# Attention with beacons, then a multiplicative feed-forward: the order of the weight loads, of the weight fusion and of the first two batches

## The chip, the cores and the metric

One Trainium2 chip, one core. The metric is device time of one launch in microseconds (us), the median of repeated runs. Everything below runs in one program: five engines (TensorE or PE, VectorE or DVE, ScalarE or ACT, GpSimd or POOL, SyncE or SP), each with its own instruction queue, and DMA queues that are fed from POOL and from SP.

## The reference

There are 8 batches of 8 heads with 576 positions of 64 elements, and 16 beacon positions in front of keys and values. Attention is causal over the positions, and the beacons are open to all. Its output, with the heads side by side, is the token matrix x of 4608 rows and 512 columns of a feed-forward without any nonlinearity but a product:

```python
k_all = np.concatenate([beacon_k, k], axis=2)
v_all = np.concatenate([beacon_v, v], axis=2)
scores = scale * np.matmul(q, k_all.transpose(0, 1, 3, 2))
scores = np.where(causal, -1000000000.0, scores)
a = np.exp(scores - scores.max(-1, keepdims=True))
a /= a.sum(-1, keepdims=True) + 1e-09
attn = np.matmul(a, v_all)
x = attn.transpose(0, 2, 1, 3).reshape(B * S, H * D)
h = (x @ w1) * (x @ w2) @ w3
out = h @ w_out
```

w1 and w2 are 512 x 1024, w3 is 1024 x 1024, w_out is 1024 x 512. All inputs and the output are float32.

## The kernel before

**Attention.** A batch is worked through in eight steps, two for each pair of heads (`t`), the even one for the first half of the column groups, the odd one for the second (lines 340 to 411). A step consists of `scores` (L351, eight or fourteen matmuls of 64 rows, two heads in two halves of the array), two `exps` on ScalarE (L360), one or two masks on VectorE (L372), `values` (L389, six or twenty-four matmuls of 65 columns; the 65th column of v is one and gives the sum), and a reciprocal and a multiplication on VectorE (L397, L398) that write the normalised rows into x16. Scores lie transposed (keys on partitions), so that the exponentials feed `values` without a transpose.

**Layout of q and k.** Batches 0 and 1 take a path of their own: `load_pair` brings float32 pairs of heads into the tile `st` (L138; batch 0 from SP's queue, batch 1 from POOL's), `cast_pair` casts them on VectorE (L157), and `pe_transpose_pair` transposes them on PE (L171), with the copy of qT on VectorE and that of kT on ScalarE (L177). Batches 2 to 7 are loaded by POOL with a cast to float16 (L104, L113) and transposed by DMAs that SP issues (`transpose_qk`, L128 and L129), five chunks of q and five of k. The rows of x are transposed on PE for batches 0 and 1 (`pe_transpose_x`, L187) and by SP's DMAs later (L409).

**Feed-forward.** w3 @ w_out is computed once, as Wt (`fuse`: for each of eight row tiles eight transposes of w3, L254, a copy on VectorE, L256, eight matmuls of 512 columns, L264, and a copy to float16 on ScalarE, L273). Then x is handled in nine chunks of 512 rows. `ff_ab` has 64 matmuls of 512 columns (L284): eight times a group of four for w1, whose result ScalarE copies into a_sb (L295), and a group of four for w2, which VectorE multiplies with it into gT (L297). `ff_out` has 32 matmuls with Wt (L305), four copies to an output tile `ot` on VectorE (L315, three buffers), and four output DMAs from SP (L316). All products go through the three PSUM buffers of the tile `pm`, which the transposes on PE use as well. w3 is loaded into columns of xT that batches from 4 on will fill (L240).

**Order.** The order on every engine is that of the program text. The feed-forward is a generator, `stream`, that yields after each of its matmuls (64 for the fusion, 96 for each chunk, 928 in all), and `emit_ff(n)` takes the next n of them. The list `fill` says how many are taken in each step. The main loop (L453 to L494) writes scores and the first exponential of step s + 1, then values of step s, up to eight matmuls of the feed-forward, the second exponential and the first mask of step s + 1, the rest of the fill, and the second mask. The last lines of a step add loads of v for the next batch and of q and k for the one after it (at the first step of a batch) and the transposes by DMA (steps 1 to 5).

At the start, POOL's queue holds v of batch 0, w_out, w3, w1 and w2, then q and k of batch 1 in `st`, its v, and q and k of batch 2. Batch 0's attention runs one step ahead of its values. Eight matmuls of the fusion follow step 6 and the other 56 step 7, with the transposes of batch 0's x between; then the first 28 matmuls of the product of chunk 0 surround the transposes of batch 1's pairs. Batch 1 takes 58 more in its steps, batches 2 to 7 take 536, and the remainder follows the last step:

```python
LEFT = 50
n_first = 28
n_kept = 10
n_second = 96 - n_first - n_kept
...
rest, n = n_kept + 6 * 96 - LEFT, NS - 2 * NSB
```

Of the kernel before, what the change touches and what calls it, by code (L numbers as in the profile page):

```python
# [39 lines left out]
def kernel(  # L40
# [81 lines left out]
    def load_v(b, jt):  # L122
        load_kv(b, jt, v, beacon_v, vas[b % NB2][:, jt, :, 0:64])
# [8 lines left out]
    early_qk, early_b = {}, {}  # L132

    def load_pair(b, t):
        engine = nc.gpsimd if b else nc.sync
        for i, src in enumerate((q, k)):
            st = early.tile([P, 2, RUN * D], FP32, name="st")
            engine.dma_start(  # L138
                st[:NR], src[b, ds(2 * t, 2)].rearrange("h (p j) d -> p h (j d)", j=RUN)
            )  # L140
            early_qk[b, t, i] = st
        if t == 0:
            bst = bkp.tile([Nb, H, D], FP32, name="bst")
            engine.dma_start(bst, beacon_k[b].rearrange("h n d -> n h d"))
            early_b[b] = bst

    o16s = {}
# [1 line left out]
    def cast_pair(b, t):  # L149
        if t == 0:  # L150
            b16 = bkp.tile([Nb, DM], FP16, name="b16")
            nc.vector.tensor_copy(b16, early_b[b].rearrange("p h d -> p (h d)"))
            early_b[b] = b16
        o16s[t] = []
        for i in range(2):
            o16 = tiny.tile([P, RUN, P], FP16, name=f"o16_{i}")
            nc.vector.tensor_copy(  # L157
                o16[:NR].rearrange("p j (h d) -> p h j d", h=2),
                early_qk[b, t, i][:NR].rearrange("p h (j d) -> p h j d", j=RUN),
            )  # L160
            o16s[t].append(o16)

    def pe_transpose_pair(b, t):
        qT, kT = qTs[b % NB2], kTs[b % NB2]
        for o16, dst, off, copy in (
            (o16s[t][0], qT, 0, nc.vector.tensor_copy),
            (o16s[t][1], kT, Nb, nc.scalar.copy),
        ):
            pt = psM.tile([P, 1024], FP16, name="pm")
            for j in range(RUN):  # L170
                nc.tensor.transpose(pt[:, ds(j * NR, NR)], o16[:NR, j, :], ident[:NR, :NR])  # L171
            if off:
                nc.tensor.transpose(
                    pt[:, ds(S, Nb)], early_b[b][:, ts(t, P)], ident[:Nb, :Nb]
                )
                copy(dst[:, t, 0:Nb], pt[:, ds(S, Nb)])
            copy(  # L177
                dst[:, t, ds(off, S)].rearrange("p (i j) -> p i j", j=RUN),
                pt[:, 0:S].rearrange("p (j i) -> p i j", j=RUN),
            )  # L180

    def pe_transpose_x(b):
        for i in range(NJT):
            pt = psM.tile([P, NT, P], FP16, name="pm")
            n = QTN[i]
            for t in range(NT):
                nc.tensor.transpose(  # L187
                    pt[:, t, 0:n], x16s[b][:n, i, ts(t, P)], ident[:n, :n]
                )
            dst = xT[:, :, ds(b * S + QT0[i], n)]  # L190
            if i % 2:
                nc.scalar.copy(dst, pt[:, :, 0:n])
            else:
                nc.vector.tensor_copy(dst, pt[:, :, 0:n])

    nc.vector.memset(ident, 1.0)
    nc.vector.memset(MA, 1.0)
# [35 lines left out]
        )  # L233
    for c in range(NJT):
        load_v(0, c)
    wo_v = moe_w_out.rearrange("(a c p) n -> a p c n", p=P, c=2)
    for a in range(4):
        nc.gpsimd.dma_start(wo16[:, ds(2 * a, 2), :], wo_v[a])

    w316 = xT[:, :, ds(M // 2, 2 * DF)].rearrange("p a (c r) -> p a c r", c=2)  # L240
    for kt in range(NFT):
        nc.gpsimd.dma_start(w316[:, kt // 2, kt % 2], moe_w3[ts(kt, P), :])
    for c in range(4):
        for i, w in enumerate((moe_w1, moe_w2)):
            nc.gpsimd.dma_start(
# [4 lines left out]
    def fuse():  # L250
        def w3_transposed(kt):
            pt = psM.tile([P, NFT, P], FP16, name="pm")
            for rt in range(NFT):
                nc.tensor.transpose(pt[:, rt, :], w316[:, kt // 2, kt % 2, ts(rt, P)], ident)  # L254
            wT = wp.tile([P, NFT, P], FP16, name="wT")
            nc.vector.tensor_copy(wT, pt)  # L256
            return wT

        wT = w3_transposed(0)
        for kt in range(NFT):  # L260
            nxt = w3_transposed(kt + 1) if kt + 1 < NFT else None
# [12 lines left out]
            wT = nxt  # L274
            yield
# [64 lines left out]
    def scores(s):  # L340
        b, t, half = s // (2 * NT), (s // 2) % NT, s % 2
        if half == 0:
            pTs[s // 2] = ptp.tile([P, 2, PW], FP16, name="pT")
        qT, kT = qTs[b % NB2], kTs[b % NB2]
        pss[s] = []
        for g in (2 * half, 2 * half + 1):
            ps = psS.tile([P, 2, 512], FP32, name="ps")
            pss[s].append(ps)
            for jt, q0, n, col in GROUPS[g]:
                for hh in range(2):  # L350
                    nc.tensor.matmul(  # L351
                        ps[:, hh, ds(col, n)],
                        kT[ds(hh * 64, 64), t, ts(jt, P)],
                        qT[ds(hh * 64, 64), t, ds(q0, n)],
                    )
# [64 lines left out]
    fill[6] = 8  # L420
    for s in range(NSB, 2 * NSB):
        fill[s] = n_second * (s - NSB + 1) // NSB - n_second * (s - NSB) // NSB
    rest, n = n_kept + 6 * 96 - LEFT, NS - 2 * NSB
    for s in range(2 * NSB, NS):
        fill[s] = rest * (s - 2 * NSB + 1) // n - rest * (s - 2 * NSB) // n

    cast_pair(0, 0)
# [12 lines left out]
    constants(1)  # L440
    for i in range(NB2):
        nc.vector.memset(k16s[i][64:128, 4, :], 0.0)
        nc.vector.memset(q16s[i][64:128, 4, :], 0.0)
    for t in range(2):
        load_pair(1, t)
    for c in range(NJT):
        load_v(1, c)
    for t in range(2, NT):
        load_pair(1, t)
    for c in range(NJT):  # L450
        load_q(2, c)
        load_k(2, c)
    for s in range(NS):  # L453
        b, r = s // NSB, s % NSB
        if s == NSB - 1:
            values(s)
            emit_ff(16)
            pe_transpose_x(0)
            emit_ff(64 - emitted)
            cast_pair(1, 0)  # L460
            for t in range(NT):
                emit_ff(n_first // NT)
                pe_transpose_pair(1, t)
                if t + 1 < NT:
                    cast_pair(1, t + 1)
            emit_ff(64 + n_first - emitted)
            scores(s + 1)
            for j in range(2):
                exps(s + 1, j)
                mask(s + 1, j)  # L470
            continue
# [12 lines left out]
        if s == 2 * NSB - 1:  # L484
            pe_transpose_x(1)
        if 1 <= b < B - 1:
            if r == 0:
                for c in range(NJT):
# [37 lines left out]
```

## Time and profile before

| | |
|---|---|
| median of 8 runs | 326.35 us (323.6 to 329.66) |
| the profiled execution | 323.6 us |
| its span, first to last instruction | 321.6 us |
| PE, DVE, ACT, POOL busy | 290.7, 168.3, 157.8, 114.0 us |
| granted clock of TensorE | 1.00 |
| first product of the feed-forward (L284) | 50.4 us |
| first scores of batch 1 | 61.7 us |
| first values of batch 2 | 89.4 us |
| last matmuls of attention | about 262.8 us |
| read from and written to HBM | 39.32 MB, 9.44 MB |

Times in the trace count from the first instruction of the span. A line of the page's second part is the span in 40 slices of 8.04 us; a digit is the busy share in tenths. A line of the table of windows has the window, its length, then for PE, PE's weight loads, DVE, ACT and POOL the busy time and the number of instructions, then TensorE's granted clock, the DMA share (both kinds of queue added, so it can exceed 1) and GB/s. A line of the chain of waits has start, length, and what the end of the program hung on in that time. A line of the timeline has start, length, engine, line of the kernel, operation, output<-inputs and count; in square brackets stands the idle time before it and what ended it.

### The profile page before, as it was taken

Reading aid. Unit: us, or ns where it says so; the run is one execution under the profiler, and the core shown is the slowest. Engines: PE = TensorE matmul, PEld = TensorE weight load, DVE = VectorE, ACT = ScalarE, POOL = GpSimd, SP = SyncE. Lnnn points to the kernel's source line nnn. Section 1 sums busy time; section 2 is a strip of 40 time slices with the busy share of each in tenths; the row PEclk is TensorE's granted clock in tenths of the full one; section 3 lists DMA queues with packets and bytes.
Section 4 is the critical chain, followed back from the end, with each engine's and each line's share of the span. In section 5 each row is a group of like instructions: output and inputs, shape, how many; then the busy total and the mean of one; then the engine's idle time right before and its main releaser. Section 6 shows DMA issues by size and latency. Waiting matters only on the chain.

```text
span 321.6 us, 6961 instructions
## 1 busy us (share of the span) xinstructions
PE 290.7 (90%) x2800; PEld 151.6 (47%) x2800; DVE 168.3 (52%) x387; ACT 157.8 (49%) x229; POOL 114.0 (35%) x152
## 2 busy tenths in 40 slices
PE   1787799698999995999999999899999989999995
PEld 1565554344554452445454545454445544444442
DVE  4756435655655553555654655555645653343342
ACT  1575424577466653556466556554764452230320
POOL 8545569955593067305910960320000000000000
PEclk9999999999999999999999999999999999999999
DMA  8999999999999979997999999997451112202103
GB/s 190 212 208 205 196 222 202 135 128 139 154 188 145 132 82 178 172 151 88 197 171 170 112 207 169 119 163 143 88 75 67 65 40 62 107 0 88 42 2 130
DMA packets 155824, 42.97 MB, mean 134 GB/s; under 512 B 142976, under 2 KB 149632, under 8 KB 155792
## 3 DMA queue, kind: packets, MB, share of 16 engines
q0 software_dynamic: 102912, 19.67, 77.0%
q1 hardware_dynamic: 52880, 22.85, 39.5%
q8 instruction: 22, 0.36, 0.5%
q14 instruction: 10, 0.08, 0.1%
HBM read 39.32 MB, written 9.44 MB: 152 GB/s over the span
## 4 chain that ended last, share of the span: by engine, by line
PE 59%; DMA 21%; ACT 5%; DVE 4%; POOL 4%; issue 3%; SPq 1%; DVEq 0%; POOLq 0%
PE pm L284 29%; PE pm L305 16%; PE pv L389 8%; DMA w<-in_moe_w_dram 6%; PE ps L351 6%; ACT pT L360 3%; DMA k<-in_k_dram 3%; DMA va<-in_v_dram 3%; DMA xT<-in_moe_w_dram 3%; DMA qT<-q 2%; DMA out_dram<-ot 2%; POOL va L113 2%; DMA st<-in_k_dram 2%; ACT a_sb L295 2%; DVE gT L297 2%
## 5 line engine op out<-in xcount | busy, mean ns | idle before, releaser
L284 PE MATMUL pm<-xT,w 128*128 128x512 f16 x576 | 132.8, 379 | 1.4 <-DMA xT<-x 1.3
L360 ACT ACTIVATE pT<-ps 128x736 f16<-128x736 f32 (+3 forms) x128 | 105.9, 864 | 35.8 <-PE ps L351 35.1
L295 ACT ACTIVATE a_sb<-pm 128x512 f32<-128x512 f32 x72 | 43.0, 597 | 85.7 <-PE pm L284 83.8
L284 PEld LDWEIGHTS <-w 128*128 128x128 f16 x576 | 53.4, 98 | 60.4 <-issue 2.4
L297 DVE TENSOR_TENSOR gT<-pm,a_sb 128x512 f16<-128x512 f32 x72 | 49.7, 690 | 43.8 <-PE pm L284 42.6
L305 PE MATMUL pm<-Wt,gT 128*128 128x512 f16 x288 | 66.4, 379 | 0.0
L113 POOL DMA_DIRECT2D va<-in_v_dram x40 | 34.8, 880 | 68.4 <-PE pv L389 63.6
L351 PE MATMUL ps<-qT,kT 64*128 64x80 f16 (+3 forms) x704 | 40.3, 237 | 9.3 <-ACT pT L360 7.8
L389 PE MATMUL pv<-va,pT 128*128 128x65 f16 x960 | 42.6, 197 | 5.5 <-DVE pT L372 4.9
L389 PEld LDWEIGHTS <-pT 128*128 128x128 f16 x960 | 34.4, 99 | 15.9 <-DVE pT L372 9.9
L305 PEld LDWEIGHTS <-gT 128*128 128x128 f16 x288 | 27.0, 98 | 29.8 <-DVE gT L297 0.2
L397 DVE RECIPROCAL rd<-pv 128x4 f32<-128x4 f32 x64 | 12.1, 190 | 52.8 <-PE pv L389 52.7
L351 PEld LDWEIGHTS <-kT 64*128 64x128 f16 x704 | 21.8, 97 | 37.4 <-issue 33.5
L315 DVE TENSOR_SCALAR ot<-pm 128x512 f32<-128x512 f32 x36 | 24.8, 690 | 24.6 <-PE pm L305 20.0
L398 DVE TENSOR_TENSOR x<-pv,rd 128x256 f16<-128x256 f32 x64 | 31.4, 491 | 2.4
L104 POOL DMA_DIRECT2D q<-in_q_dram x30 | 26.0, 865 | 6.2 <-DMA va<-in_v_dram 2.8
L113 POOL DMA_DIRECT2D k<-in_k_dram x30 | 26.1, 870 | 5.4 <-DMA q<-in_q_dram 2.3
L372 DVE TENSOR_TENSOR pT<-pT,MB 128x512 f16<-128x512 f16 x64 | 19.2, 325 | 5.8 <-ACT pT L360 5.8
L171 PE MATMUL pm<-ident,o 96*128 96x96 f16 x96 | 7.6, 242 | 9.8 <-DVE o L157 8.2
L264 PE MATMUL pm<-wo,wT 128*128 128x512 f16 x64 | 15.0, 379 | 0.4 <-DVE wT L256 0.4
L372 DVE TENSOR_TENSOR pT<-pT,MA 128x480 f16<-128x480 f16 x32 | 12.7, 398 | 1.4 <-ACT pT L360 1.4
L273 ACT CAST Wt<-pm 128x512 f16<-128x512 f32 x8 | 4.7, 587 | 16.2 <-PE pm L264 16.2
(41 smaller groups left out, 94.9 us busy)
## 6 DMA issues: line engine op xcount, KB each, us to landing
out_dram<-ot SPq DMA_DIRECT2D x36, 256.0 KB, 2.7
va<-in_v_dram POOLq DMA_DIRECT2D x24, 128.0 KB, 6.6
q<-in_q_dram POOLq DMA_DIRECT2D x24, 128.0 KB, 8.0
k<-in_k_dram POOLq DMA_DIRECT2D x18, 128.0 KB, 8.8
xT<-in_moe_w_dram POOLq DMA_DIRECT2D x8, 256.0 KB, 10.1
w<-in_moe_w_dram POOLq DMA_DIRECT2D x8, 256.0 KB, 10.2
st<-in_q_dram SPq DMA_DIRECT2D x4, 288.0 KB, 5.4
st<-in_k_dram SPq DMA_DIRECT2D x4, 288.0 KB, 6.4
```

What stands on the lines that cost most here:

```text
L104: nc.gpsimd.dma_start(q16s[b % NB2][:rows, c, :].rearrange("s (h d) -> s h d", h=H), q[b, :, ds(c * P, rows), :].rearrange("h s d -> s h d"),)
L113: nc.gpsimd.dma_start(dst[ds(p0, rows)], src[b, :, ds(s0, rows), :].rearrange("h s d -> s h d"))
L284: nc.tensor.matmul(pm, w12[:, kt, ds(i * DF + kf * P, P)], xT[:, kt, ds(mc * 512, 512)], start=(kt == 0), stop=(kt == NKT - 1),)
L295: nc.scalar.activation(a_sb, pm, AF.Copy, scale=GS)
L297: nc.vector.tensor_tensor(gT[:, kf, :], pm, a_sb, ALU.mult)
L305: nc.tensor.matmul(pm, gT[:, kf, ts(mt, P)], Wt[:, kf, :], start=(kf == 0), stop=(kf == NFT - 1),)
L315: nc.vector.tensor_scalar(ot, pm, float(1.0 / GS), None, ALU.mult)
L351: nc.tensor.matmul(ps[:, hh, ds(col, n)], kT[ds(hh * 64, 64), t, ts(jt, P)], qT[ds(hh * 64, 64), t, ds(q0, n)],)
L360: nc.scalar.activation(pT[:, :, ds(GO[g], GW[g])], pss[s][j][:, :, 0 : GW[g]], AF.Exp, scale=scale)
L372: nc.vector.tensor_tensor(blk, blk, m.unsqueeze(1).to_broadcast([P, 2, n]), ALU.mult)
L389: nc.tensor.matmul(pv[:, 2 * n + hh, 0:65], pT[:, hh, ds(col, P)], va[:, jt, 2 * t + hh, 0:65], start=(jn == 0), stop=(jn == len(BLK[i]) - 1),
L398: nc.vector.tensor_tensor(x16[:, ds(tiles[0], ni), ds(t * P, P)].rearrange("p i (h d) -> p i h d", h=2), pv[:, 0 : 2 * ni, 0:64].rearrange ...
```

## The change

The change moves loads, the fusion and parts of the first two batches.

- **Loads.** After v of batch 0, POOL's queue holds w1 and w2, v of batch 1, q and k of batch 2, v of batch 2, and only then w_out and w3, followed by q and k of batch 3. Batch 1's pairs are loaded by SP's queue, once a one-element memset on VectorE has written each `st` tile; these memsets stand after step 1 of batch 0.
- **Order of the products.** The generator first yields the 64 matmuls of `ff_ab` for chunk 0, then for chunk 1, then the fusion, then both `ff_out`, then chunks 2 to 8 as before. 30 of chunk 0's matmuls surround the transposes of batch 1's pairs, 34 lie in batch 1's steps, 594 in batches 2 to 7, and 270 follow. In the fusion the next row tile's transposes are written after the fourth matmul rather than ahead of the first.
- **Batch 0.** Scores and exponentials run two steps ahead of the values, with no fusion between.
- **Spin.** 32 matmuls of zeros into a `pm` tile that nobody reads: ten at the start, two ahead of each of scores 0, scores 1, the eight values of batch 0 and the transposes of its x.
- **Small ones.** The copy of qT of batch 0's pair 1 moves to ScalarE; four memsets of the rest rows of q16 and k16 move from VectorE to POOL.

```diff
     def load_pair(b, t):
-        engine = nc.gpsimd if b else nc.sync
         for i, src in enumerate((q, k)):
             st = early.tile([P, 2, RUN * D], FP32, name="st")
-            engine.dma_start(
+            if b:
+                nc.vector.memset(st[0:1, 0, 0:1], 0.0)
+            nc.sync.dma_start(
...
-            (o16s[t][0], qT, 0, nc.vector.tensor_copy),
+            (o16s[t][0], qT, 0, nc.vector.tensor_copy if b or t != 1 else nc.scalar.copy),
...
+    def spin(n):
+        pm = psM.tile([P, 512], FP32, name="pm")
+        for _ in range(n):
+            nc.tensor.matmul(pm, zeros[:, 0:P], zeros)
...
     for c in range(NJT):
         load_v(0, c)
-    wo_v = moe_w_out.rearrange("(a c p) n -> a p c n", p=P, c=2)
-    for a in range(4):
-        nc.gpsimd.dma_start(wo16[:, ds(2 * a, 2), :], wo_v[a])
-
-    w316 = xT[:, :, ds(M // 2, 2 * DF)].rearrange("p a (c r) -> p a c r", c=2)
-    for kt in range(NFT):
-        nc.gpsimd.dma_start(w316[:, kt // 2, kt % 2], moe_w3[ts(kt, P), :])
+    for i in range(NB2):
+        nc.gpsimd.memset(k16s[i][64:128, 4, :], 0.0)
+        nc.gpsimd.memset(q16s[i][64:128, 4, :], 0.0)
     for c in range(4):
         for i, w in enumerate((moe_w1, moe_w2)):
...
-            nxt = w3_transposed(kt + 1) if kt + 1 < NFT else None
...
+                if rt == 3 and kt + 1 < NFT:
+                    nxt = w3_transposed(kt + 1)
...
     def stream():
+        gTs = []
+        for mc in range(2):
+            gTs.append((yield from ff_ab(mc)))
         yield from fuse()
-        for mc in range(M // 512):
+        for mc in range(2):
+            yield from ff_out(mc, gTs[mc])
+        for mc in range(2, M // 512):
             gT = yield from ff_ab(mc)
             yield from ff_out(mc, gT)
...
-    LEFT = 50
-    n_first = 28
-    n_kept = 10
-    n_second = 96 - n_first - n_kept
+    LEFT = 270
+    n_first = 30
+    n_second = 64 - n_first
...
+    spin(10)
     cast_pair(0, 0)
     pe_transpose_pair(0, 0)
     cast_pair(0, 1)
-    scores(0)
-    for j in range(2):
-        exps(0, j)
+    spin(2)
+    ahead(0)
     pe_transpose_pair(0, 1)
     cast_pair(0, 2)
-    for j in range(2):
-        mask(0, j)
+    masks(0)
+    spin(2)
+    ahead(1)
     pe_transpose_pair(0, 2)
     cast_pair(0, 3)
+    masks(1)
     pe_transpose_pair(0, 3)
     constants(1)
...
+    for s in range(NSB):
+        if s + 2 < NSB:
+            ahead(s + 2)
+        spin(2)
+        values(s)
+        if s + 2 < NSB:
+            masks(s + 2)
+        if s == 1:
+            for t in range(NT):
+                load_pair(1, t)
+    for c in range(NJT):
+        load_v(2, c)
+    wo_v = moe_w_out.rearrange("(a c p) n -> a p c n", p=P, c=2)
+    for a in range(4):
+        nc.gpsimd.dma_start(wo16[:, ds(2 * a, 2), :], wo_v[a])
+
+    w316 = xT[:, :, ds(M // 2, 2 * DF)].rearrange("p a (c r) -> p a c r", c=2)
+    for kt in range(NFT):
+        nc.gpsimd.dma_start(w316[:, kt // 2, kt % 2], moe_w3[ts(kt, P), :])
+    cast_pair(1, 0)
+    spin(2)
+    pe_transpose_x(0)
+    for t in range(NT):
+        emit_ff(n_first // NT)
+        pe_transpose_pair(1, t)
+        if t + 1 < NT:
+            cast_pair(1, t + 1)
+    emit_ff(n_first - emitted)
+    ahead(NSB)
+    masks(NSB)
+    for s in range(NSB, NS):
```

`ahead(s)` writes `scores(s)` and both `exps(s, j)`, `masks(s)` both masks. The branch of the main loop for the last step of batch 0 goes, and v of batch 2 is no longer loaded in batch 1's first step.

More of the change, by code (lines that the diff above doesn't have):

```diff
@@ L143, in load_pair @@
             bst = bkp.tile([Nb, H, D], FP32, name="bst")
-            engine.dma_start(bst, beacon_k[b].rearrange("h n d -> n h d"))
+            nc.sync.dma_start(bst, beacon_k[b].rearrange("h n d -> n h d"))
             early_b[b] = bst
@@ L194, in pe_transpose_x @@
                 nc.vector.tensor_copy(dst, pt[:, :, 0:n])
+    zeros = const.tile([P, 512], FP16, name="zeros")
+    nc.vector.memset(zeros, 0.0)
+    def spin(n):
+        pm = psM.tile([P, 512], FP32, name="pm")
+        for _ in range(n):
+            nc.tensor.matmul(pm, zeros[:, 0:P], zeros)
     nc.vector.memset(ident, 1.0)
@@ L414, with ahead, masks @@
     NS = B * NSB
-    LEFT = 50
-    n_first = 28
-    n_kept = 10
-    n_second = 96 - n_first - n_kept
+    LEFT = 270
+    n_first = 30
+    n_second = 64 - n_first
     fill = [0] * NS
-    fill[6] = 8
     for s in range(NSB, 2 * NSB):
         fill[s] = n_second * (s - NSB + 1) // NSB - n_second * (s - NSB) // NSB
-    rest, n = n_kept + 6 * 96 - LEFT, NS - 2 * NSB
+    rest, n = 64 + 96 * (M // 512) - 64 - LEFT, NS - 2 * NSB
     for s in range(2 * NSB, NS):
         fill[s] = rest * (s - 2 * NSB + 1) // n - rest * (s - 2 * NSB) // n
+    def ahead(s):
+        scores(s)
+        for j in range(2):
+            exps(s, j)
+    def masks(s):
+        for j in range(2):
+            mask(s, j)
+    spin(10)
     cast_pair(0, 0)
@@ L429 @@
     cast_pair(0, 1)
-    scores(0)
-    for j in range(2):
-        exps(0, j)
+    spin(2)
+    ahead(0)
     pe_transpose_pair(0, 1)
     cast_pair(0, 2)
-    for j in range(2):
-        mask(0, j)
+    masks(0)
+    spin(2)
+    ahead(1)
     pe_transpose_pair(0, 2)
     cast_pair(0, 3)
+    masks(1)
     pe_transpose_pair(0, 3)
     constants(1)
[L441 to L445, printed above, removed]
     for c in range(NJT):
         load_v(1, c)
-    for t in range(2, NT):
-        load_pair(1, t)
     for c in range(NJT):
@@ L452 @@
         load_k(2, c)
-    for s in range(NS):
-        b, r = s // NSB, s % NSB
[L455 to L471, printed above, removed]
+    for s in range(NSB):
[28 more added lines that the diff above has]
+    for s in range(NSB, NS):
+        b, r = s // NSB, s % NSB
         if s + 1 < NS:
@@ L487 @@
             if r == 0:
-                for c in range(NJT):
+                for c in range(NJT if b > 1 else 0):
                     load_v(b + 1, c)
```

## The prediction

> **What bounds the kernel now.** I read the page's 40 slices first, then the table of windows, then the chain of waits and the timeline of TensorE. The slices say where the time is lost:
>
> ```profile
> PE   1787799698999995999999999899999989999995
> DMA  8999999999999979997999999997451112202103
> GB/s 190 212 208 205 196 222 202 135 128 139 154 188 145 132 82 178 172 151 88 197 171 170 112 207 169 119 163 143 88 75 67 65 40 62 107 0 88 42 2 130
> ```
>
> A slice is 8.04 us. TensorE (PE) has holes in the first eleven slices and is nearly full afterwards; the DMA engines are full until about 225 us. The windows, cut where the stages change, count the matmuls:
>
> ```profile
> 15.10:50.37 35.27, 30.90 (x349) 19.64 (x349) 17.62 (x48) 16.96 (x25) 20.50 (x30) 1.00 1.39 207
> 50.37:61.73 11.36, 9.69 (x81) 5.28 (x79) 8.38 (x13) 5.11 (x11) 10.43 (x13) 1.00 1.76 171
> 61.73:89.20 27.47, 24.28 (x307) 13.20 (x308) 14.87 (x40) 18.40 (x26) 16.44 (x22) 1.00 1.90 145
> ```
>
> Busy time is no measure, because a 512-column matmul is recorded with 379 ns but the chain passes 32 of them in 6.91 us, 0.216 us each. Attention costs PE 0.98 us per step, half of 0.48 + 0.20 + 0.45 + 0.83 (scores and values of an even and an odd step). The chain:
>
> ```profile
> 14.20 8.72 DMA xT<-in_moe_w_dram
> 23.21 19.25 DMA w<-in_moe_w_dram x2
> ...
> 84.05 0.48 PE ps L351 x8
> 84.53 0.83 PE pv L389 x24
> ...
> 269.47 6.91 PE pm L305 x32
> ```
>
> The reader is to see in the first two lines that the end hangs on w3 (it lies in xT) and then on w1 and w2: the first product comes at 50.4 us, batch 1's scores at 61.7. The first values matmul of batch 2 starts at 89.36 ("t2"):
>
> ```profile
> 88.91 0.52 PE L351 MATMUL ps<-qT,kT 64*128 64x128 f16 x14
> 89.36 0.35 PE L389 MATMUL pv<-va,pT 128*128 128x65 f16 x6
> 89.55 2.32 PE L305 MATMUL pm<-Wt,gT 128*128 128x512 f16 x10
> ```
>
> From t2 on I make a balance. By then 150 of the 928 matmuls that the generator yields ("items") are out: 64 + 28 + 58. Left are 778 x 0.216 = 168.0 us; 48 steps x 0.98 = 47.0; 3.75 from the last matmul to the end. Sum 218.8; real 321.6 - 89.4 = 232.2. So 13.4 us are stalls: 3.6 between 123.5 and 128.5 (output tiles waiting for their DMAs) and 9.8 over 48 steps, 0.20 a step, mostly scores waiting for an exponential that stood behind a product copy on ScalarE.
>
> **What the Trainium skill says.** "TensorE: Matmul & The Clock Gate", Part 1, has PE at half rate after an idle window of about 3.4 us. The trace agrees in the matmuls, though not in the clock column (1.00 throughout): the same 24 values matmuls take 1.50 us at 17.93, 1.08 at 26.00, 0.90 later. "DMA: Bandwidth & Descriptors", Specifications, gives about 358 GB/s of HBM per core: w_out, w3, w1 and w2, 10.5 MB of source, came in from 13.9 to 42.5 us, 367 GB/s. The same section wants 512 bytes a transfer for line rate: the page counts 142,976 of 155,824 packets under that, and q, k and v of one batch (3.54 MB) take 20.6 us (first issue of v 60.98 to last of k 81.58), half the rate of the weights. Its section on queues, rings and completion order says that an engine alternates between queues by packet: at the start SP's pairs and GpSimd's v landed together, 13.7 and 13.9 us.
>
> **The change, part by part.**
>
> *Batch 0 without fusion, two steps ahead.* ScalarE becomes the pace: 16 exponentials x 0.84 = 13.4, plus the copies of kT of pairs 1 to 3 (0.81 each) and the qT copy of pair 1 that moves to it (0.64). The first starts at 9.2 as before, and I allow 0.5 for gaps at the first pairs: 9.2 + 13.4 + 2.4 + 0.6 + 0.5 = 26.1; the last mask, values and normalisation add 2.0: 28.1 (before: 34.0). DVE needs about 1.3 of each 1.7 us step. The 32 spin matmuls: ten run from about 1.6 to 5.9 (0.427 each at half rate, an estimate from the skill's page), ahead of the first transposes at 6.6; the 20 between steps lie where PE waits for ScalarE. I price them at 0; if that cover were gone, 20 x 0.216 = 4.3. Two stand ahead of x's transposes: 0.4. They may also give back up to 1 us of half-rate time; I take none.
>
> *Memsets.* Four leave DVE (4 x 0.27) for POOL. POOL shows no such row: between 0 and, by its 128-column select of 0.29, 1.2 us each, so at most 4.7. POOL would be free for w1 at 12.9, and v still occupies the ring until 13.9: 0. The eight one-element memsets on DVE cost at most 0.09 each (the smallest rows are 0.07 to 0.09), but they hold batch 1's SP loads until step 1 is through, about 20 us.
>
> *Loads.* w1, w2 (4.2 MB) and batch 1's q, k (2.36 MB) follow v: 6.55 MB at 0.367 MB/us is 17.9, so both have landed at 32; the pairs at 26 to 32. x's transposes start at 28.5 and end at 31. Then pairs and 30 items as before: 50.4 to 61.7 held 28, so 11.3 + 0.4: batch 1's scores at 42.7. The pairs are wanted at 31, 34, 37, 40: no wait.
>
> *Batch 1.* 34 items in place of 58. Before: 61.7 to 89.4, 27.7 us. 24 x 0.216 = 5.2 can go; but ScalarE needs 4.0 a pair of steps (4 x 0.84 + 0.6) and each product copy keeps its place in the chain of exponentials, so I take 4.1: 23.6. **t2 becomes 66.3**, 23.1 earlier.
>
> *After t2.* 864 items are left: 186.6. The 64 w3 transposes, at 2.17 us a row less 1.73, cost 8 x 0.44 = 3.5. Attention 47.0, tail 3.75: 240.9. The balance is 22.1 heavier than before, so **work and head start nearly cancel and the stalls decide**. Steps: 12.4 items in place of 11.2; the first eight stand ahead of the second exponential, so the cover behind it grows from 3.2 to 4.4 items (0.69 to 0.95 us): stall from 0.20 to 0.10 a step, 4.8; bounds 2 and 10. Outputs: chunks 0 and 1 put eight in a row into batch 3, among ten transposes of 1.3 us issue each on SP; three output buffers: 2 us, where 3.6 stood before (bounds 0 and 5). LEFT only moves items behind the last step.
>
> *Loads after 32.* GpSimd's queue holds v1 and q, k of batch 2 (its share without transposes beside it about 15 a set, then 20.6): v1 at 38, q and k 51; their last SP transpose (1.3 issue, 7.2 landing) 59.5, wanted at 62. Then v2 at 58, w_out and w3 (6.3 MB) at 75, wanted by the fusion 64 items into batch 2 at 86. q, k of batch 3 stand behind them: 89, transposed at 97.5. They are wanted seven steps after t2: 87 items 18.8, 7 x 0.98, 2.2 of transposes, 0.7: 94.8. Stall 3 (bounds 0 and 10); v3 follows at 96, and the exponentials give it time.
>
> Sum: 66.3 + 240.9 + 4.8 + 2 + 3 = **317.0** of span. The profiled execution took 323.6 for its 321.6, so 319.0; it was the lowest of the eight runs (median 326.35), so 319.0/323.6 = 0.986 of the median: **321.7**, 1.4% less.
>
> **The rivals.** *Slower: the weights push batch 3's q and k too far back.* At 23 us a set (issue at 85.66 to landing at 108.5): v1 40, q and k 55, transposed 64 against 62 (t2 68.3), v2 63, weights 80.5, q and k of batch 3 at 96, transposed 104.5 to 105 against 96.8: 8 us. 317.0 + 2 + 5 = 324: 329 by the same ratio. It decides from a landing of about 102. For it: the slices full for the first 225 us. Against: the same bytes, and a batch then lasts 29 us.
> *No change:* the casts of batch 1 wait for SP's loads, or batch 1 keeps its 27 us of chain; t2 at 71: 321.7, so 326. For it: batch 1's steps are latency, not work.
> *Larger gain:* batch 1 at ScalarE's pace (4 x 4.0, t2 62.7), stall 0.05 a step, no other: 62.7 + 240.9 + 2.4 + 1 = 307; 311.6. For it: PE follows ScalarE alone then. Against: the product copy between the exponentials stays.
> *That the change does not do what it says:* the instruction order of the built kernel has the loads, products and fusion moved as stated, so I leave it out.
>
> **How the numbers follow.** Forecast 0.48, slower 0.20, no change 0.15, larger gain 0.17. The range runs from the larger gain's end to past the slower case: 312 to 330. A measurement of this kernel tells 0.5% from no change, 324.7 to 328.0. Faster: 0.42 of the forecast, 0.17, 0.03 of no change: 0.62. Same: 0.05, 0.10, 0.03: 0.18. Slower: the rest, 0.20.
>
> **What would show it.** First product near 31 us; batch 1's scores near 43; first values of batch 2 near 66; if that is over 71, the head start failed. PE's wait for batch 3's qT or kT tells forecast from slower rival. Wait of scores for the exponentials shows the stall a step. A wait of the fusion for w3 or w_out, or of output tiles beyond 5 us, would prove my queues wrong.

## The result and the profile after

The changed kernel takes 322.38 us (median of 20 runs, 319.51 to 324.71) against 326.39 (57 runs of the kernel before, 323.6 to 331.7). The ratio is 0.9876, with a 95% interval from 0.9853 to 0.9898: 1.2% faster. The forecast was 321.7 us, 0.986 of the median before. Ratios here and below leave out the few runs in which the chip was in a slower state (one of the 20 of the changed kernel, 324.71 us); medians have all runs. The profiled execution took 323.17 us, with a span of 321.1, so it is one of the slower ones of the changed kernel, as the profiled one of the kernel before is its fastest; the two spans differ by 0.5 us only, and stages are compared below rather than spans.

The page of the changed kernel, in the same 40 slices (8.03 us each now):

```profile
PE   6897868899989999699999999999999999999995
...
PEclk9789999999999999899999999999999999999999
DMA  8999999999999999999999999944700430202103
GB/s 181 203 197 264 197 140 155 156 210 177 143 135 155 146 154 162 244 142 165 140 135 161 158 149 160 171 85 112 141 12 4 127 77 25 108 0 86 47 0 131
```

The first slices of TensorE look alike (they count the spins now), but what is done in them is not the same, as the windows show. The hole that the kernel before had in the 16th slice (120 to 128 us, a 5) is gone; there is a new one in the 17th (128 to 136 us, a 6), and in it the granted clock reads 8. The DMA engines are full for 26 slices, 209 us, rather than 28, without the slices of 7 that they had before.

The windows, cut at the same events as before (end of batch 0, first scores of batch 1, first values of batch 2):

```profile
28.94:45.14 16.20, 12.93 (x129) 7.53 (x130) 11.60 (x21) 6.14 (x14) 8.72 (x11) 1.00 1.80 188
45.14:68.98 23.84, 19.33 (x285) 11.08 (x285) 13.09 (x37) 17.89 (x26) 12.07 (x19) 1.00 1.63 167
```

Batch 1's scores come at 45.1 us where they came at 61.7; its steps last 23.8 us where they lasted 27.6. The first values of batch 2, the point t2 of the prediction, in the timeline of TensorE:

```profile
68.53 0.52 PE L363 MATMUL ps<-qT,kT 64*128 64x128 f16 x14
68.98 0.35 PE L401 MATMUL pv<-va,pT 128*128 128x65 f16 x6
69.17 2.76 PE L291 MATMUL pm<-xT,w 128*128 128x512 f16 x12
```

69.0 us instead of 89.4, so 20.4 earlier. The chain of waits now hangs on other transfers:

```profile
18.00 19.45 DMA va<-in_v_dram
...
51.32 13.63 DMA wo<-in_moe_w_out_dram
...
66.05 10.20 DMA xT<-in_moe_w_dram
...
123.84 9.09 DMA qT<-q
...
133.06 0.39 PE ps L363 x4
```

This is GpSimd's queue of loads in the new order, v of batch 1, then w_out and w3, and behind it, at 124 us, the transposes for batch 4. The hole in slice 17 is the end of that chain, in the timeline of TensorE:

```profile
130.10 0.33 PE L363 MATMUL ps<-qT,kT 64*128 64x128 f16 x4
133.06 0.39 PE L363 MATMUL ps<-qT,kT 64*128 64x256 f16 x4 [2.63 <-DMA qT<-q]
133.39 0.97 PE L401 MATMUL pv<-va,pT 128*128 128x65 f16 x24
134.17 3.18 PE L312 MATMUL pm<-Wt,gT 128*128 128x512 f16 x7
137.14 1.64 PE L291 MATMUL pm<-xT,w 128*128 128x512 f16 x6
```

The scores of batch 4's first step wait 2.63 us for qT. Then seven matmuls take from 134.17 to 137.14, about 0.424 us each in place of 0.216: TensorE ran at half rate after the pause, which is another 1.5 us. From values of step 30 to values of step 32 it takes 11.94 us, where the pairs of steps on both sides of it take 7.3 to 7.6 and the same pair takes 7.45 in e2, e3 and e5 below: 4.5 us lost.

What TensorE waited for between t2 and the last step, first in the kernel before (89 to 263 us), then in the changed one (68.9 to 255.6); columns are the total, the number of waits and the longest:

```profile
PE ps L351 <- ACT pT L360: 4.5, 9, 1.0
PE pv L389 <- DVE pT L372: 2.1, 1, 2.1
PE pm L284 <- DMA xT<-x: 1.3, 1, 1.3
PE ps L351 <- DMA qT<-q: 0.4, 1, 0.4
```

```profile
PE ps L363 <- DMA qT<-q: 2.6, 1, 2.6
PE ps L363 <- ACT pT L372: 2.0, 6, 0.5
PE pm L269 <- DVE wT L262: 1.0, 1, 1.0
```

The wait for exponentials has more than halved. In the kernel before, the 2.1 us for a mask are a wait for an output tile in disguise: VectorE, which works in order, stands before the tile, and the mask comes behind it:

```profile
127.49 0.69 DVE L315 TENSOR_SCALAR ot<-pm 128x512 f32<-128x512 f32 x1 [4.50 <-DMA out_dram<-ot]
128.10 0.40 DVE L372 TENSOR_TENSOR pT<-pT,MA 128x480 f16<-128x480 f16 x1
128.55 0.35 PE L389 MATMUL pv<-va,pT 128*128 128x65 f16 x6 [2.15 <-DVE pT L372]
```

That wait is gone in the changed kernel, and one for qT has taken its place.

### The profile page after: what moved, and what is told of

The parts are those of the page before. It is cut to its first block, busy times and chain, and to the rows that moved or that the text cites. A ratio compares the mean times of both kernels' runs of the same rounds, so it can differ in the third digit from the quotient of the medians.

```text
span 321.1 us, 7027 instructions
## 1 busy us (share of the span) xinstructions
PE 297.6 (93%) x2832; PEld 152.0 (47%) x2832; DVE 167.1 (52%) x391; ACT 158.6 (49%) x230; POOL 110.5 (34%) x147
## 3 DMA queue, kind: packets, MB, share of 16 engines
q0 software_dynamic: 102240, 17.28, 78.5%
## 4 chain that ended last, share of the span: by engine, by line
PE 55%; DMA 25%; POOL 12%; issue 4%; ACT 2%; DVE 0%; POOLq 0%
PE pm L291 29%; PE pm L312 16%; DMA q<-in_q_dram 6%; DMA va<-in_v_dram 6%; PE pv L401 6%; PE ps L363 5%; DMA wo<-in_moe_w_out_dram 4%; POOL va L113 4%; DMA xT<-in_moe_w_dram 3%; DMA qT<-q 3%; POOL k L113 2%; POOL w L251 2%; DMA k<-in_k_dram 2%; POOL q L104 2%; ACT pT L372 1%
## 5 line engine op out<-in xcount | busy, mean ns | idle before, releaser
L312 PE MATMUL pm<-Wt,gT 128*128 128x512 f16 x288 | 67.4, 385 | 0.0
L363 PE MATMUL ps<-qT,kT 64*128 64x80 f16 (+3 forms) x704 | 37.8, 232 | 9.2 <-ACT pT L372 6.5
L401 PE MATMUL pv<-va,pT 128*128 128x65 f16 x960 | 41.5, 194 | 1.4 <-DVE x L410 0.8
L401 PEld LDWEIGHTS <-pT 128*128 128x128 f16 x960 | 33.7, 98 | 12.6 <-issue 3.7
L363 PEld LDWEIGHTS <-kT 64*128 64x128 f16 x704 | 21.1, 95 | 37.5 <-issue 35.6
L113 POOL DMA_DIRECT2D k<-in_k_dram x30 | 25.4, 847 | 13.3 <-DMA va<-in_v_dram 6.4
L269 PE MATMUL pm<-wo,wT 128*128 128x512 f16 x64 | 16.4, 380 | 1.0 <-DVE wT L262 1.0
L204 PE MATMUL pm<-zeros 128*128 128x512 f16 x32 | 11.5, 474 | 1.3 <-DVE zeros L199 1.3
L158 DVE CAST o<-st 96x768 f16<-96x768 f32 x16 | 10.6, 690 | 1.4 <-PE pm L204 0.6
```

The source lines that it names most:

```text
L113: nc.gpsimd.dma_start(dst[ds(p0, rows)], src[b, :, ds(s0, rows), :].rearrange("h s d -> s h d"))
L312: nc.tensor.matmul(pm, gT[:, kf, ts(mt, P)], Wt[:, kf, :], start=(kf == 0), stop=(kf == NFT - 1),)
L363: nc.tensor.matmul(ps[:, hh, ds(col, n)], kT[ds(hh * 64, 64), t, ts(jt, P)], qT[ds(hh * 64, 64), t, ds(q0, n)],)
L401: nc.tensor.matmul(pv[:, 2 * n + hh, 0:65], pT[:, hh, ds(col, P)], va[:, jt, 2 * t + hh, 0:65], start=(jn == 0), stop=(jn == len(BLK[i]) - 1),
```

## The experiments

Theory: the order of the loads gives a head start, the heavier stages after t2 take most of it back, and the stalls decide; the stalls fall because more feed-forward matmuls cover each step's exponentials, and a backlog of loads, which w3 and w_out now enlarge at a later time, takes part of it again at batch 4. Rivals: that the spins or the two steps ahead make the start fast; that the wait at batch 4 is only the order of SP's queue. Each experiment is one edit of the changed kernel, with its own ratio to the kernel before on the same chip (six runs each; e7 and e8 four, e10 22). The times in the last three columns are of one profiled execution. This table collects what the timelines show; "values 32" is the first values matmul of batch 4.

| kernel | ratio [95%] | median | first product | t2 | values 32 |
|---|---|---|---|---|---|
| before | 1 | 326.39 | 50.4 | 89.4 | 150.5 |
| changed | 0.9876 [0.9853, 0.9898] | 322.38 | 33.2 | 69.0 | 139.2 |
| e1, no spins | 0.9868 [0.983, 0.9905] | 321.56 | 34.4 | 72.2 | 138.8 |
| e2, one step ahead | 0.9842 [0.9809, 0.9874] | 320.31 | 34.4 | 70.1 | 135.8 |
| e3, w3 and w_out first | 1.0082 [1.0052, 1.0112] | 328.11 | 38.3 | 78.5 | 144.2 |
| e4, transposes early | 0.9852 [0.9808, 0.9896] | 320.3 | 33.4 | 69.2 | 136.3 |
| e5, no q, k of batch 5 | 0.9836 [0.979, 0.9881] | 321.13 | 34.6 | 71.9 | 137.6 |
| e6, e2 and e4 | 0.9859 [0.9813, 0.9904] | 321.07 | 35.0 | 72.8 | 139.1 |
| e7, 334 left | 1.0141 [1.009, 1.0192] | 331.06 | 33.9 | 69.7 | 133.9 |
| e8, batch 1 empty | 1.0236 [1.0186, 1.0286] | 334.31 | 34.1 | 66.7 | 138.9 |
| e10, pairs on GpSimd | 0.996 [0.9935, 0.9984] | 324.03 | 33.7 | 69.9 | 141.1 |
| e11, 240 left | 0.9795 [0.9746, 0.9845] | 318.61 | 34.1 | 70.4 | 138.3 |
| e12, e11 and e4 | 0.9883 [0.9829, 0.9937] | 321.24 | 33.8 | 69.4 | 140.7 |
| e13, e11 and e2 | 0.9764 [0.971, 0.9818] | 319.32 | 35.1 | 71.2 | 138.1 |

**The order of the loads (e3).**

```diff
+    wo_v = moe_w_out.rearrange("(a c p) n -> a p c n", p=P, c=2)
+    for a in range(4):
+        nc.gpsimd.dma_start(wo16[:, ds(2 * a, 2), :], wo_v[a])
+
+    w316 = xT[:, :, ds(M // 2, 2 * DF)].rearrange("p a (c r) -> p a c r", c=2)
+    for kt in range(NFT):
+        nc.gpsimd.dma_start(w316[:, kt // 2, kt % 2], moe_w3[ts(kt, P), :])
     for c in range(4):
         for i, w in enumerate((moe_w1, moe_w2)):
```

The same lines are taken away behind the loads of v of batch 2.

> The changed kernel with w_out and w3 loaded ahead of w1 and w2 again, all else as changed. Theory (the head start is the order of the loads): w1 and w2 land 6.3 MB / 0.367 = 17 us later, so the first product comes at 45 to 49 us in place of 33, first values of batch 2 at 81 to 85 in place of 69; a part returns because the later stages wait less for DMAs: 332 to 338 us. Rival, the head start comes from batch 0 and the spins, not from the loads: first product before 38 us, 322 to 326 us.

Measured: 1.0082, slower than the kernel before, and 328.11 us. The first product comes at 38.3, not at 45 to 49, since it needs only the first quarter of w1 and w2; but it waits for the two quarters in turn, 4.02 and 2.22 us, as the timeline shows:

```profile
38.29 1.89 PE L298 MATMUL pm<-xT,w 128*128 128x512 f16 x4 [4.02 <-DMA w<-in_moe_w_dram]
42.40 1.46 PE L298 MATMUL pm<-xT,w 128*128 128x512 f16 x3 [2.22 <-DMA w<-in_moe_w_dram]
43.66 1.17 PE L172 MATMUL pm<-ident,o 96*128 96x96 f16 x12
```

t2 is 78.5: 9.5 us later than in the changed kernel. Of these about 4.5 come back, because batch 4's scores do not wait (values 32 are 65.7 us after t2, against 70.2). With the new order of the products, the order of the loads is worth 2.1% of the time, more than the whole change brings; the rest of the change without it is a small loss. The size was less than I expected (328.11 lies between the two ranges), the direction is the theory's. The other way round, the new loads with the fusion still ahead of the first product, was not tried, so the order of the products has no price of its own.

**Spins (e1).**

```diff
     def spin(n):
+        return
```

> The changed kernel without the 32 spin matmuls. My balance priced them at nothing: they lie in TensorE's waiting time, and the half-rate time they save in batch 0 is at most 1 us. Theory: 322.4 to 323.4 us, values of batch 0 at half rate until about 24 us as in the kernel before, but ScalarE still the pace of batch 0. Rival 1, the spins are what makes the start fast: 324.5 to 327 us, with the end of batch 0's values 2 to 4 us later. Rival 2, the spins stand in the way: 319 to 321 us.

Measured: 321.56 us, 0.9868; between the theory's range and the second rival's, and not to be told from the changed kernel. But this trace has t2 3.2 us later, and the window from 24 to 45 us shows why, first without spins, then the changed kernel:

```profile
24.00:45.00 21.00, 16.11 (x162) 10.01 (x160) 12.85 (x30) 7.53 (x13) 10.59 (x13) 0.76 1.66 203
```

```profile
24.00:45.00 21.00, 16.43 (x186) 9.49 (x184) 14.90 (x33) 8.72 (x18) 10.19 (x13) 1.00 1.67 206
```

The granted clock, the third number from the end, is 0.76 against 1.00, and 24 matmuls fewer get done, ten of them the spins themselves. One would credit the spins with 3.2 us; but e5, whose instructions are the same as the changed kernel's up to batch 3, spins included, has a clock of 0.76 from 10 to 40 us (0.92 there in the changed kernel) and t2 at 71.9:

```profile
10.00:40.00 30.00, 25.79 (x301) 15.49 (x300) 16.95 (x56) 16.86 (x27) 16.32 (x22) 0.76 1.57 210
```

The matmuls agree with the column: the first seven products take 3.15 us in e1, 3.06 in e5 and 1.67 in the changed kernel. So the half rate in the first 45 us comes and goes with the execution, with spins as well. The Trainium skill says this in "TensorE: Matmul & The Clock Gate", Part 1: the window in which activity is counted is free-running, so that the same kernel warms up at different points. Of the spins' own time nothing shows at the end, as priced; whether they shift the odds is left open. And what t2 loses here does not reach the end, because batch 4 waits less in exchange.

**Two steps ahead (e2).**

```diff
-        if s + 2 < NSB:
-            ahead(s + 2)
+        if s + 1 < NSB:
+            ahead(s + 1)
...
-        if s + 2 < NSB:
-            masks(s + 2)
+        if s + 1 < NSB:
+            masks(s + 1)
```

with `ahead(1)` and `masks(1)` taken from the start in the same way.

> The changed kernel with batch 0's scores and exponentials one step ahead of the values rather than two. Theory (the two steps ahead make ScalarE the pace of batch 0 and so end it earlier): batch 0's last values, 28.9 us in the changed kernel, come at 31 to 33, and all of it arrives at the end: 324.5 to 326.5 us. Rival, the start hangs on the loads and not on batch 0's pace: first product still near 33 us, 322 to 323 us.

Measured: 320.31 us. The theory falls: batch 0's last values move by 1.0 us only (28.94 to 29.92, the start of its 24 matmuls), t2 by 1.1, and the end is not later. Even this 1.0 is within what the half rate moves: e5, two steps ahead, has those values at 30.41. The rival is not right as put either (the first product is at 34.4, and the time is below its range). In this trace the wait at batch 4 is absent (values 30 to 32 take 7.45 us), with all loads in place; e5 below comes back to this.

**Transposes ahead of the output DMAs (e4), and both (e6).**

```diff
         values(s)
+        if 1 <= b < B - 1 and r < NJT:
+            transpose_qk(b + 1, r)
         k1 = min(8, fill[s])
...
-            if 1 <= r <= NJT:
-                transpose_qk(b + 1, r - 1)
```

> The changed kernel with the DMA transposes of the next batch's q and k written one step earlier and ahead of the step's feed-forward matmuls, so that on SP's queue they stand ahead of the output DMAs. Theory, the wait of batch 4's scores for qT (2.6 us in the trace, then some 1.5 us of half-rate matmuls) comes from SP's order, where the transposes stand behind output DMAs that wait for their tiles: the wait goes, 317.5 to 319.5 us. Rival, the loads of batch 4's q and k are late because w3 and w_out stand ahead of them on GpSimd's queue: the wait stays, 321.5 to 323 us.

> Batch 0 one step ahead (320.3 us by itself) and the transposes ahead of the feed-forward (320.3 us by itself) together. If both had only taken the same wait at batch 4 away, the sum gives nothing more: 319.6 to 320.6 us. If each gave something of its own, 318 to 319.2 us.

Measured: 320.3 and 321.07 us, e4 between its two ranges and e6 above both of its own. In e4's trace no wait for qT or kT is left, but values 31 now wait for masks (0.68 and 0.21 us): VectorE, in order, stands 2.16 us before an output tile whose DMA, issued at 123.3 us, lands 7.4 us later. From values 30 to values 32 it takes 8.7 us (127.6 to 136.3), against 11.9. VectorE stands before that tile in the changed kernel too, 2.75 us at 131.0, unseen because TensorE is waiting for qT. So issuing the transposes earlier is enough to remove the wait for them, and then the next transfer that lands late shows. Neither ratio can be told from the changed kernel's, and e6 adds nothing to e2 or e4.

**Load taken away (e5).**

```diff
-                for c in range(NJT if b + 2 < B else 0):
+                for c in range(NJT if b + 2 < B and b != 3 else 0):
```

> The changed kernel without the loads of q and k of batch 5 (batch 5 then computes with batch 3's, so its rows differ). Theory: the wait of batch 4's scores for qT comes from the DMA engines' backlog, which the weights pushed behind batch 2's loads left and which is still there at 120 us; without these 2.4 MB, which share the engines with batch 4's transposes, the transposes land in 4 us rather than 8 and the wait goes: values of step 32 at 134 to 136 us in place of 139, 317.5 to 320 us. Rival: the wait comes from SP's order alone (transposes behind output DMAs): values of step 32 still near 139, 321.5 to 323 us.

Measured: the wait at batch 4 is gone, with SP's order as it was (in the timeline):

```profile
129.74 0.52 PE L363 MATMUL ps<-qT,kT 64*128 64x128 f16 x14
130.19 0.35 PE L401 MATMUL pv<-va,pT 128*128 128x65 f16 x6
...
130.38 2.76 PE L312 MATMUL pm<-Wt,gT 128*128 128x512 f16 x12
...
133.07 0.55 PE L363 MATMUL ps<-qT,kT 64*128 64x128 f16 x8
133.55 0.90 PE L401 MATMUL pv<-va,pT 128*128 128x65 f16 x24
```

Batch 4's scores (133.07) follow without a pause. The transposes issued between 110 and 135 us land after a median of 2.4 and 2.5 us; in the changed kernel, the second pair of lines, it is 8.2 and 7.9:

```profile
qT<-q SPq DMA_TRANSPOSE x5, 2.4
kT<-k SPq DMA_TRANSPOSE x5, 2.5
```

```profile
qT<-q SPq DMA_TRANSPOSE x4, 8.2
kT<-k SPq DMA_TRANSPOSE x4, 7.9
```

By itself this run does not show the cause, because its t2 is 2.9 us later and e2 and e3 have no wait either, with every load in place. What these three share is that the loads were out of the way. From t2 to values 30 all of them and the changed kernel take the same 58.24 us; in the changed kernel the loads of batch 5's q and k, which stand at the end of the backlog, land until 133.9 us, when batch 4's scores (130.1) already wait, and in e2 until 123.5. The median landing of the transposes in the same window in e2:

```profile
qT<-q SPq DMA_TRANSPOSE x4, 4.1
kT<-k SPq DMA_TRANSPOSE x4, 3.1
```

e10, where these loads land until 138.2, waits longest at batch 4, 3.7 us. In e1, where t2 is even later than in e5 (72.2) and they land until 130.8, 0.7 us are left. So the wait needs two things, transposes that are issued late (behind the output DMAs, e4) and a backlog of loads beside which they land slowly (e5, e2); either taken away removes it. Why the same loads end ten microseconds later in the changed kernel's execution than in e2's, these traces do not tell.

The time of e5, 321.13 us, lies above what I put down, with t2 at 71.9 in the profiled execution and a wait of 1.1 us at batch 5; its ratio cannot be told from the changed kernel's.

**How many matmuls a step carries (e7, e11).**

```diff
-    LEFT = 270
+    LEFT = 334
```

This is e7; e11 has 240 in the same place.

> The changed kernel with 334 matmuls of the feed-forward left for after the last step rather than 270, so 11.0 in a step in place of 12.4. Theory, the start of batch 4 is set by the DMA engines: the 16 steps before it get 4.6 us shorter, but values of step 32 stay at 137 to 140 us; the steps after it stall 0.05 us more each: the 13.8 us that move behind the end are not fully won back, 326 to 329 us. Rival, the wait hangs on the steps (SP's order): values of step 32 move to 134 to 135.5 us with the steps, 322.5 to 324.5 us.

> The changed kernel with 240 feed-forward matmuls left for after the last step in place of 270, 13.0 a step in place of 12.4. With 11.0 a step the steps stalled 0.36 us each, with 12.4 only 0.14. Theory (matmuls behind the second exponential cover the chain of exponentials): the stall falls to 0.08 to 0.12 a step, 1 to 3 us over 48 steps, and the longer batches give the DMA engines time, so that the wait at batch 4 shrinks: 318.5 to 321 us. Rival, the cover is complete already and the last chunks now wait for the transposes of batch 7's x: 322.5 to 325 us.

Measured: 331.06 and 318.61 us. Between values 36 and values 62, where no transfer is late, a step takes 3.646 us in the kernel before (11.2 matmuls), 3.588 in e7 (11.0), 3.796 in the changed kernel (12.4) and 3.896 in e11 (13.0). Less 0.216 for each matmul and 0.98 for attention, the stall a step is 0.25, 0.22, 0.14 and 0.11. (The 0.36 in e11's expectation was a miscount of mine; this sum gives 0.22.) The cover is real: each matmul more in a step costs about 0.16 us there (3.896 - 3.588 over 2.0 matmuls), not 0.216.

In e7, values 32 came at 133.9, about where the rival had them, but two steps later the backlog caught the kernel in another place, and the time is above either expectation:

```profile
136.66 8.52 SPq L323 DMA_DIRECT2D out_dram<-ot  x4
...
144.13 0.69 DVE L322 TENSOR_SCALAR ot<-pm 128x512 f32<-128x512 f32 x1 [4.46 <-DMA out_dram<-ot]
145.19 0.35 PE L401 MATMUL pv<-va,pT 128*128 128x65 f16 x6 [3.52 <-DVE pT L384]
```

VectorE waits 4.46 us for an output tile to be stored, the mask behind it on VectorE is late, and TensorE waits 3.52 us for the mask. e11 is the reverse: longer batches, no wait for qT, 0.8% under the changed kernel, with intervals that do not overlap.

**Batch 1 without feed-forward (e8).**

```diff
-    n_second = 64 - n_first
+    n_second = 0
...
-    rest, n = 64 + 96 * (M // 512) - 64 - LEFT, NS - 2 * NSB
+    rest, n = 64 + 96 * (M // 512) - n_first - LEFT, NS - 2 * NSB
```

> The changed kernel with no feed-forward matmuls in batch 1's steps; the 34 of them go into batches 2 to 7 (13.1 a step). Batch 1 took 3.8 us less with 24 fewer, so 0.16 us each: its 34 save 4 to 5.5 us, and first values of batch 2 come at 63.5 to 65 in place of 69. Theory, batch 4's start is set by the DMA engines: values of step 32 stay at 137 to 141 us, and the 34 matmuls come on top in part: 324.5 to 327 us. Rival, no such limit: values of step 32 at 132 to 134 us, 321.5 to 323.5 us.

Measured: 334.31 us, worse than both. t2 comes 2.3 us earlier only. This execution began batch 1 1.2 us later (46.3 us against 45.1), so batch 1 itself got 3.4 us shorter (20.4 against 23.8), and its 34 matmuls cost 0.10 us each. One reason is that TensorE without them falls to half rate, as the window of batch 1 in e8 shows (granted clock 0.77; it is 1.00 there in the changed kernel):

```profile
45.00:67.00 22.00, 17.19 (x266) 12.01 (x266) 11.00 (x34) 17.03 (x23) 10.80 (x17) 0.77 1.74 156
```

The steps of batch 1 are latency, and what is put there costs less than half of its own time. Of the 2.3 nothing is left: the scores of batch 3 (at 93 us) and a product that stands before an output tile (at 146 us) wait,

```profile
PE pm L291 <- DVE ot L322: 5.2, 1, 5.2
PE ps L363 <- DMA qT<-q: 3.5, 1, 3.5
```

and values 32 stand at 138.9, as in the changed kernel. The number is the theory's, the place is not: batch 4 does not wait here (values 30 to 32 take 7.67 us, with 13.1 matmuls a step); the DMA engines stopped batch 3 instead, and the price was higher than I said.

**Batch 1's pairs on GpSimd's queue (e10).**

```diff
-            if b:
-                nc.vector.memset(st[0:1, 0, 0:1], 0.0)
-            nc.sync.dma_start(
+            (nc.gpsimd if b else nc.sync).dma_start(
...
+    for t in range(NT):
+        load_pair(1, t)
     for c in range(NJT):
         load_v(1, c)
...
-        if s == 1:
-            for t in range(NT):
-                load_pair(1, t)
```

> The changed kernel with batch 1's pairs loaded by GpSimd's queue behind w1 and w2 again (no memset, no SP loads), v of batch 1 behind them. Theory (what the head start needs is that w1, w2 and the pairs come ahead of w3 and w_out; which queue issues the pairs matters little, since TensorE wants them between 31 and 41 us): first product 32 to 35 us, v of batch 1 some 3 us later than in the changed kernel and just in time, 321.5 to 325 us. Rival, SP's loads beside GpSimd's are what gives the start its speed: first values of batch 2 at 73 us or later in place of 69, 326 to 330 us.

Measured: 324.03 us, in the theory's range: first product 33.7, t2 69.9. SP's loads are not what makes the start fast. But its ratio, 0.996, is 0.8% above the changed kernel's, and the trace has the wait at batch 4 larger (3.7 us for qT; values 30 to 32 take 12.9): everything on GpSimd's queue stands later.

**Combinations (e12, e13).** e12 is e11's edit with e4's, e13 is e11's with e2's.

> 240 left and the transposes ahead of the feed-forward together: a version that might beat both kernels. Theory: the wait at batch 4 goes and the steps stall less, 317.5 to 319.5 us. Rival, both only remove the same wait, so that nothing adds: 319.5 to 321 us.

> 240 left (318.6 us, no wait at batch 4) and batch 0 only one step ahead. Theory: where the wait at batch 4 is gone, nothing absorbs a head start any more, so that the 1.1 us by which two steps ahead brought first values of batch 2 forward reach the end: 319.3 to 320.3 us. Rival, the two steps ahead are worth nothing: 318 to 319 us.

Measured: 321.24 and 319.32 us. e12 is above both ranges: with the transposes ahead, a mask stands behind an output tile, as in e4, values wait 2.67 us for it, and the 13 matmuls after that take 4.6 us in place of 2.8, at half rate for a part again. On the same chip all of its runs (320.25 us and up) are slower than all of e11's (319.79 and less). e13's median lies at the edge of the theory's range, but its chip ran the kernel before slower too: by ratio e13 is at 0.9764, e11 at 0.9795. Their intervals overlap, so that two steps ahead are worth nothing that these runs can tell, though the trace has t2 0.8 us earlier with them. e11 and e13 beat both kernels of the study.

## Why the prediction was right, step by step

The direction, the size (0.986 forecast, 0.9876 measured) and the account (head start against heavier stages, decided by stalls) held; where the stalls fall did not. By its steps:

- **Head start.** Forecast t2 66.3, trace 69.0; forecast gain 23.1, measured 20.4. The error is 2.1 us at the first product (31 forecast, 33.15 measured), 0.3 in the 30 matmuls with the pairs and 0.2 in batch 1 (23.6 forecast, 23.8 measured). Most of it, 1.6 us, is batch 0: x's transposes were to start at 28.5 and start at 30.1, and then two of them wait for copies on ScalarE. That batch 0 ends early was credited to the two steps ahead, and with one step ahead it ends no more than 1.0 us later (e2). Of the 20.4, the order of the loads carries 9.5 (e3); no run divides the other 10.9 between the fusion, which no longer stands ahead of the first product, and batch 1's 34 matmuls in place of 58.
- **Loads.** The queue was forecast well: v of batch 1, q and k of batch 2, w3 and q and k of batch 3 at 38, 51, 75 and 89 us, landed by 40.6, 51.0, 77.5 and 87.7; the fusion, which wanted w3 at 89.5, did not wait for it. The rate it rests on was misread: v of batch 0 had landed by 16.1 us, not by 13.9 (its second chunk), so the 10.5 MB of weights came at 397 GB/s rather than 367, farther above the 358 that the prediction sets beside it. The pairs of batch 1 landed by 37.9, not 32, while v of batch 1 was loaded beside them; each was wanted late enough.
- **Balance after t2.** Forecast 240.9 of work, as before plus 22.1; the trace has 252.1 from t2 to the end, so 11.2 of stalls, forecast 9.8, 13.4 before. About 6.7 of them are the steps (48 x 0.14), 4.5 the wait at batch 4.
- **Steps.** The fall by 0.10 that I took from the cover of 4.4 instead of 3.2 matmuls was measured as 0.11 (0.25 to 0.14), and e7 and e11 move it both ways.
- **Output tiles.** Forecast 2 us; no wait of TensorE for them in this trace. e7 and e8 show that it stands close to them: 3.5 and 5.2 us. In the kernel before, 1.3 of the 3.6 us that the prediction put down to output tiles were products that waited for a transpose of x.
- **Batch 3's q and k.** Forecast: transposed at 97.5, wanted at 94.8, a stall of 3. Measured: wanted at 98.2, since t2 was later, and no wait at all. In e8, whose t2 of 66.7 is close to the forecast's 66.3, the wait is there, 3.5 us. The slower rival had the right mechanism (w3 and w_out push q and k back), but in the changed kernel's trace the queue caught up with TensorE one batch later, at batch 4, for 4.5 us with the half-rate matmuls, which the forecast did not have. My sum had said that after batch 3 the longer batches would give time; but GpSimd's last k of the backlog was issued at 121 us and landed at 133.9, and until then a transpose took 8 us rather than 2.4.
- **Spins, memsets.** Priced at 0. The spins: nothing to be told at the end (e1). The four memsets on POOL took from 8.5 to 11.6 us and w1 was issued at once; whether they cost anything was not tried by itself.
- **A sum that does not come out.** The larger gain's t2 of 62.7 is 4.0 us more than its own 4 x 4.0 after 42.7, which is 58.7; the prediction does not say where they come from.

That the median came within 0.2% owes something to luck. The span that was summed, 317.0 us, is 4.1 short of the trace's 321.1: t2 came 2.7 late, and the stalls were 1.4 more (1.9 more in the steps, 4.5 for a wait that was not forecast, less 3 and 2 for two that did not come). The median hides this, because the forecast went from span to median by way of the fastest execution of the kernel before (323.6 us, 2.75 under its median), while the profiled execution of the changed kernel is one of its slower ones (323.17, 0.8 above its median). Which execution is profiled is chance: with the half rate in the first 45 us, t2 moves by 2.9 us between the traces of the changed kernel and of e5, whose instructions are the same that far.

Left open: whether the wait at batch 4 comes in every execution of the changed kernel. All of its 20 runs but the slowest spread over 4.2 us, the six of e2, whose trace shows none, over 1.9; each trace is of one execution.

## What to carry to other kernels

Order loads by the first use of what they bring, and let the work that needs the last of them run later beside something else; but follow the displaced bytes to the place where they come to stand, which here was batch 4. In a stage whose steps are chains of latency, filling matmuls cost much less than their own time (0.10 us of 0.216 in batch 1, 0.16 in the later steps), so it pays to spread them there rather than leave them for the end. When a backlog has to be paid, reordering the queue that waits only showed the next late transfer here and brought nothing that can be told (e4), and with longer steps it cost time (e12 against e11); giving the stage time (e11) did bring something.

## What the runs showed of the hardware

- A pause of TensorE of 2.63 us was followed by 3 us of matmuls at half rate (0.424 us for 512 columns), pauses of 2.67 us in e12 and of 3.51 us in e8 likewise, so a wait of this length cost more than its length. After 1.84 us in e7 (11 matmuls of 512 columns in 2.54 us) and 2.15 us in the kernel before (11 in 2.54) it did not.
- A DMA transpose issued by SP landed after a median of 2.4 us when GpSimd's loads were out of the way (e5) and of 8 us beside them (changed kernel), with a median issue time of 1.2 to 1.4 us in both.
- The half rate in the first 45 us varied between executions of the same instructions (changed kernel and e5), by 2.9 us at t2, although matmuls of zeros were there to keep TensorE busy.
